# An MLP behind a layer norm: three tiles of the first block transposed before their normalisation, which moves behind the matmul as row and column corrections

## The chip, the cores and the metric

One core of a Trainium2 chip. The core has five engines that run side by side and meet at semaphores: TensorE (PE, matmuls, with its weight loads shown as PEld), VectorE (DVE), ScalarE (ACT), GpSimd (POOL) and SyncE (SP, which here only issues DMA transfers). The metric is device time in microseconds. Before the change the median of three runs is 398.32 us (398.21 to 398.36).

## The reference

```python
B, S, D, F = 1, 2048, 1024, 3584          # bfloat16 inputs

def _layernorm(x, axis=-1, eps=1e-5):
    m = jnp.mean(x, axis=axis, keepdims=True)
    v = jnp.var(x, axis=axis, keepdims=True)
    return (x - m) / jnp.sqrt(v + eps)

def reference(x, w1, b1, w2, b2):
    y = _layernorm(x, axis=-1)
    h = _gelu(jnp.einsum("bsd,df->bsf", y, w1) + b1)
    return jnp.einsum("bsf,fd->bsd", h, w2) + b2
```

## The kernel before

The 2048 rows of x are 16 tiles of 128, in four blocks of four tiles (512 rows). For each block the kernel normalises the four tiles, transposes them into yT_sb (model dimension on the partitions, eight chunks dt of 128), computes mm1, 28 rows r of 128 hidden units (eight matmuls of 512 columns each, summed in one bank of PSUM), applies gelu on ScalarE into hT_sb, and computes mm2, eight groups of 28 matmuls, which VectorE adds b2 to and SyncE stores. Blocks 1 to 3 are normalised and transposed by VectorE (in 32 by 32 pieces, L355) while TensorE works on the block before.

Block 0 has nothing to hide behind, and its opening is written out by hand. It is called the wave here: mm1 of the first seven rows, each in a PSUM bank of its own (ps_1 banks 0 to 4, ps_2 banks 1 and 0), taken in cells of one tile, one row and one chunk dt (128 columns), in an order that follows the arrival of tiles and weights. There are 4 x 7 x 8 = 224 cells (L415). Its transposes are done by TensorE (L378, 128 by 128, into a free bank) and copied to yT_sb by ScalarE (L385). The wave's order of cells and transposes comes from WAVE_K, T_PUTS and GROUPS; each engine runs its list in the order written. After the wave come rows 7 to 27 with 512 columns per matmul; row 7 is in the bank ps_t (which the transposes used before), row 8 in ps_1 bank 0, and so on round six banks, so that a row waits for the gelu of the row that had its bank.

Tile 0 is normalised in a special way: VectorE takes the statistics of its first half (L264), ScalarE sums its second half with one activation (L494), VectorE adds the two to four times the mean (L275) and writes 4x - 4m to o_sb (L281); tile 1 is centred by its mean alone (L286). TensorE starts on tile 0 then. For these two tiles the factor 1/deviation, a vector over rows of x and thus over columns of yT, is applied in PSUM: VectorE spreads it over the partitions by 16 small transposes (rbc_sb, L337) and multiplies 256 columns of each of block 0's 28 mm1 rows by it before the gelu (L425, dve_scale). Tiles 2 and 3 are normalised fully (L290), with the deviation's power of -1/2 on GpSimd (L268).

Until tile 0 is ready TensorE runs matmuls of ones (L490): 34 ungated, three behind tile 0's mean, and three more after the first five transposes. Loads go out on two queues: ScalarE's first issues x0's second half and all of x1; SyncE's issues x0's first half, then w0 to w5 (w1's rows 0 to 6, one 128-row chunk dt each, 224 KB), the halves of x2, w6, w7, the halves of x3, b1, and the larger rest.

A planner puts VectorE's later work in order before the launch: ops of `crit` (the scalings of block 0 and the additions of b2) and of `fill` (the next block's statistics and transposes) are merged by estimated due times, which start from T_DVE_START and T_PE_START. VectorE runs them in that order and waits at each for its semaphores.

Of the kernel before, what the change touches and what calls it, by code (L numbers as in the profile page):

```python
# [5 lines left out]
ACT = mybir.ActivationFunctionType  # L6
# [5 lines left out]
P = 128  # L12
# [3 lines left out]
K_GROUPS = 2  # L16
NB1 = 5
# [3 lines left out]
WARM_A = ((34, None), (3, "m4"))  # L21
WARM_B = 3
N_CENTRED = 2
T_PUTS = {0: (None, None, 6), 1: (21, 35), 2: (96, 118), 3: (140, 156)}
NORM = {0: (0, 2, 8), 1: (0, 4, 8), 2: (0, 4, 8)}
GROUPS_0 = (0, 2, 5, 8)
WAVE_ROWS_0 = 6
WAVE_K = (0, 2, 4, 5, 6, 8)
GROUPS_1 = (0, 4, 8)
# [61 lines left out]
def bass_standalone__mixer_channel_mlp__prompt_kernel(  # L91
# [53 lines left out]
    with ExitStack() as es:  # L145
# [67 lines left out]
        def issue(item):  # L213
            if item[0] == "x" and item[-1] in "ab":
# [44 lines left out]
        pool.op(lambda e: e.memset(b1r_sb[:, :], 0.0), sig="b1z")  # L259
        dve.op(lambda e: e.memset(st_sb[:, :, 12:14], 0.0))  # L260
# [6 lines left out]
        def op_aggr(i):  # L267
            pool.op(lambda e, i=i: e.tensor_tensor(out=rstd_sb[:, i:i + 1], in0=mv_sb[:, i, 1:2],  # L268
                                                   in1=nhalf[:, i:i + 1], op=ALU.pow),
                    waits=[f"mv{i}", "nhalf"], sig=f"rstd{i}")  # L270
            return (lambda e, i=i: e.bn_aggr(mv_sb[:, i, :], st_sb[:, i, :]),  # L271
                    [f"st{i}_0", f"st{i}_1", "eps"], f"mv{i}", 0.33)

        def op_mean0():
            return (lambda e: e.tensor_scalar(out=m4_sb[:, :], in0=st_sb[:, 0, 1:2], scalar1=st_sb[:, 0, 4:5],  # L275
                                              scalar2=half_sb[:, :], op0=ALU.add, op1=ALU.add),
                    ["st0_0", "half"], "m4", 0.1)

        def op_norm(i, c0, c1, sig):
            if i == 0:  # L280
                return (lambda e, c0=c0, c1=c1: e.tensor_scalar(  # L281
                            out=o_sb[:, 0, c0:c1], in0=x_sb[:, 0, c0:c1], scalar1=4.0,
                            scalar2=m4_sb[:, :], op0=ALU.mult, op1=ALU.subtract),
                        ["m4"], sig, 0.02 + (c1 - c0) * 0.00055)
            if i < N_CENTRED:
                return (lambda e, i=i, c0=c0, c1=c1: e.tensor_scalar(  # L286
                            out=x_sb[:, i, c0:c1], in0=x_sb[:, i, c0:c1], scalar1=mv_sb[:, i, 0:1],
                            scalar2=None, op0=ALU.subtract),
                        [f"mv{i}"], sig, 0.02 + (c1 - c0) * 0.00055)
            return (lambda e, i=i, c0=c0, c1=c1: e.tensor_scalar(  # L290
                        out=x_sb[:, i, c0:c1], in0=x_sb[:, i, c0:c1], scalar1=mv_sb[:, i, 0:1],
                        scalar2=rstd_sb[:, i:i + 1], op0=ALU.subtract, op1=ALU.mult),
                    [f"rstd{i}", f"mv{i}"], sig, 0.02 + (c1 - c0) * 0.00055)
# [3 lines left out]
        def ops_norm(i):  # L297
            cuts = NORM.get(i, (0, DT))
# [27 lines left out]
        def ops_rbc():  # L326
            res = []
            for i in range(N_CENTRED):
                res.append((lambda e, i=i: e.tensor_scalar(out=rq_sb[:, i, :], in0=ones[:, 0:32],
                                                           scalar1=rstd_sb[:, i:i + 1], scalar2=(1.0 if i else 0.25),  # L330
                                                           op0=ALU.mult, op1=ALU.mult),
                            ["ones", f"rstd{i}"], f"rq{i}", 0.1))
            for tq in range(4):
                for q in range(4):
                    src = rq_sb[32 * tq:32 * (tq + 1), :, :]
                    dst = rbc_sb[32 * q:32 * (q + 1), :, 32 * tq:32 * (tq + 1)]
                    res.append((lambda e, src=src, dst=dst: e.transpose(out=dst, in_=src), [f"rq{N_CENTRED - 1}"],  # L337
                                ("rbc" if tq == 3 and q == 3 else None), 0.1))
            return res
# [4 lines left out]
        def ops_T(i):  # L344
            blk, t = divmod(i, TPB)
            waits = [y_ev[i][-1]]
            if blk - 2 in mm1_done:
                waits.append(mm1_done[blk - 2])
            res = []
# [15 lines left out]
        t_banks = [("t", ps_t[:, 0, :]), ("2_0", ps_2b[:, 0, :]), ("t", ps_t[:, 0, :])]  # L365

        def pe_T(i, groups, k):
            blk, t = divmod(i, TPB)
            j0, j1 = groups[k], groups[k + 1]
            bname, bap = t_banks[k if i == 0 else 0]  # L370
            evs = yT_ev.setdefault(i, [None] * DT)
            for j in range(j0, j1):
                waits = []
                if j == j0:
                    waits = ["ident"] + ([bank_read[bname]] if bname in bank_read else [])
                if j == j0 or y_ev[i][j] != y_ev[i][j - 1]:
                    waits.append(y_ev[i][j])
                pe.op(lambda e, i=i, j=j, o=(j - j0) * P, bap=bap: e.transpose(  # L378
                    out=bap[:, o:o + P], in_=(x_sb[:, i] if i else o_sb[:, 0])[:, j * P:(j + 1) * P],
                    identity=ident[:, :]),  # L380
                    waits=waits, sig=(f"tp{i}_{k}" if j == j1 - 1 else None))
                evs[j] = f"te{i}_{k}"
            src = bap[:, 0:(j1 - j0) * P].rearrange("p (j s) -> p j s", j=j1 - j0)
            dst = yT_sb[:, blk % 2, j0:j1, t * P:(t + 1) * P]
            act.op(lambda e, dst=dst, src=src: e.copy(out=dst, in_=src), waits=[f"tp{i}_{k}"], sig=f"te{i}_{k}")  # L385
            bank_read[bname] = f"te{i}_{k}"
            pe_t[0] += (j1 - j0) * 0.056
# [240 lines left out]
```

## Time and profile before

| | |
|---|---|
| median of three runs | 398.32 us |
| span of the profiled execution, first to last instruction | 396.9 us |
| what lies around the span (median less span; the profile gives no other time of that execution) | 1.42 us |
| TensorE busy | 394.1 us (99%) |
| VectorE, ScalarE, GpSimd busy | 152.8, 82.8, 9.7 us |
| wave, first cell to row 7's first matmul | 5.92 to 20.00 us |
| mm2 of block 0, first matmul | 56.42 us |

A timeline row gives the start in us, the length in us, the engine, the line, the operation with its output and inputs, the count, and in brackets the idle time before it and what ended that. A row of the chain of waits gives start, length, engine, output tile, line and count. A row of a group gives line, engine, operation, shapes and count, then busy us and mean ns of one, then the idle time before. A DMA row gives what is moved, the queue, the count, the size and the us from issue to landing. A matmul's length includes its passage through the array, so the pace is read from starts.

### The profile page before, as it was taken

The numbers are of one execution on the slowest core, as the hardware profiler recorded it, in microseconds if no ns is written. First come the engines' busy times: TensorE is split into PE (matmuls) and PEld (weight loads), VectorE is DVE, ScalarE is ACT, GpSimd is POOL, SyncE is SP. The second block draws the span as 40 slices with busy tenths as digits, with TensorE's granted clock in tenths as the row PEclk, the third lists the DMA queues.
The fourth block names the chain that finished last, engine by engine and source line by source line (L and its number), as shares of the span: only waits on it lengthen the run. The fifth ranks groups of instructions, "written<-read, shape, count | busy, mean of one in ns | idle before, by whom it ended". The sixth has DMA issues, their size and how long they took to land.

```text
span 396.9 us, 4883 instructions
## 1 busy us (share of the span) xinstructions
PE 394.1 (99%) x2116; PEld 191.7 (48%) x2116; DVE 152.8 (38%) x345; ACT 82.8 (21%) x124; POOL 9.7 (2%) x24
## 2 busy tenths in 40 slices
PE   9999999999999999999999999999999999999998
PEld 8944444444444444444444444444444444444447
DVE  5847899989998005988100000001100000001011
ACT  4273430000133442000024433100003334400000
POOL 2101000020002000000000000000000000000000
PEclk9999999999999999999999999999999999999999
DMA  8999940000000000000000000000000000000000
GB/s 286 347 380 384 387 154 13 26 29 13 26 2 0 2 0 1 28 13 26 28 13 0 2 0 2 13 13 28 16 24 15 0 0 2 0 13 28 13 28 26
DMA packets 16924, 23.64 MB, mean 60 GB/s; under 512 B 1672, under 2 KB 10504, under 8 KB 16904
## 3 DMA queue, kind: packets, MB, share of 16 engines
q1 hardware_dynamic: 16616, 22.95, 16.4%
q8 instruction: 16, 0.26, 0.3%
q10 hardware_dynamic: 288, 0.39, 0.3%
q14 instruction: 4, 0.03, 0.0%
HBM read 19.14 MB, written 4.19 MB: 59 GB/s over the span
## 4 chain that ended last, share of the span: by engine, by line
PE 99%; ACT 0%; DVE 0%; issue 0%
PE ps L466 49%; PE ps L415 41%; PE ps_t L415 8%; PE ps L490 1%; PE ps_t L378 0%; ACT yT_sb L385 0%; DVE o_sb L477 0%
## 5 line engine op out<-in xcount | busy, mean ns | idle before, releaser
L466 PE MATMUL ps<-w_sb,hT_sb 128*128 128x512 bf16 (+1 forms) x980 | 194.2, 361 | 0.0
L415 PE MATMUL ps<-yT_sb,w_sb 128*128 128x512 bf16 (+1 forms) x920 | 167.4, 340 | 0.1
L466 PEld LDWEIGHTS ps<-w_sb,hT_sb 128*128 128x128 bf16 x980 | 91.3, 98 | 102.7
L415 PEld LDWEIGHTS ps<-yT_sb,w_sb 128*128 128x128 bf16 x920 | 80.9, 98 | 82.5 <-issue 0.3
L432 ACT ACTIVATE hT_sb<-ps,b_sb 128x512 bf16<-128x512 f32 x94 | 64.0, 688 | 237.2 <-PE ps L415 217.1
L477 DVE TENSOR_TENSOR o_sb<-ps,b_sb 128x512 bf16<-128x512 f32 (+1 forms) x35 | 22.6, 646 | 198.2 <-PE ps L466 198.1
L355 DVE STREAM_TRANSPOSE yT_sb<-x_sb 32x256 bf16<-32x256 bf16 x192 | 83.7, 436 | 26.6 <-PE ps_t L415 23.5
L415 PE MATMUL ps_t<-yT_sb,w_sb 128*128 128x512 bf16 x144 | 34.0, 379 | 0.0
L264 DVE BATCH_NORM_STATS2 st_sb<-x_sb 128x6 f32<-128x512 bf16 x32 | 21.1, 674 | 4.9 <-DMA x_sb<-in_x_dram 4.9
L415 PEld LDWEIGHTS ps_t<-yT_sb,w_sb 128*128 128x128 bf16 x144 | 14.0, 98 | 16.8
L432 ACT ACTIVATE hT_sb<-ps_t,b_sb 128x512 bf16<-128x512 f32 x18 | 12.4, 690 | 17.0 <-PE ps_t L415 14.6
L425 DVE TENSOR_TENSOR ps<-ps,rbc_sb 128x256 f32<-128x256 f32 x24 | 9.7, 426 | 6.1 <-PE ps L415 5.9
L268 POOL TENSOR_TENSOR rstd_sb<-mv_sb,nhalf 128x1 f32<-128x1 f32 x16 | 8.9, 559 | 118.7 <-DVE mv_sb L271 118.7
L290 DVE TENSOR_SCALAR x_sb<-x_sb,mv_sb,rstd_sb 128x1024 bf16<-128x1024 bf16 (+1 forms) x15 | 7.8, 525 | 3.9 <-POOL rstd_sb L268 3.3
L385 ACT COPY yT_sb<-ps_t 128x512 bf16<-128x512 bf16 (+2 forms) x8 | 4.4, 545 | 8.1 <-PE ps_t L378 8.1
L490 PE MATMUL ps<-const-bfloat16-1.0 128*128 128x128 bf16 x40 | 4.6, 302 | 0.8 <-PEq L613 0.8
L490 PEld LDWEIGHTS ps<-const-bfloat16-1.0 128*128 128x128 bf16 x40 | 4.0, 139 | 1.0 <-issue 0.8
L271 DVE BATCH_NORM_AGGREGATE mv_sb<-st_sb 128x2 f32<-128x15 f32 x16 | 3.5, 221 | 1.3
L337 DVE STREAM_TRANSPOSE rbc_sb<-rq_sb 32x64 f32<-32x64 f32 x16 | 3.8, 236 | 0.2
L378 PE MATMUL ps_t<-ident,x_sb 128*128 128x128 bf16 x24 | 2.3, 219 | 0.0
L425 DVE TENSOR_TENSOR ps_t<-ps_t,rbc_sb 128x256 f32<-128x256 f32 x4 | 1.6, 405 | 0.1
L493 ACT ACT_TABLE_LOAD x1 | 1.3, 1283 | 1.7 <-PEq L613 1.7
(24 smaller groups left out, 8.0 us busy)
## 6 DMA issues: line engine op xcount, KB each, us to landing
w_sb<-in_w_dram SPq DMA_DIRECT2D x4, 1792.0 KB, 18.3
out_dram<-o_sb SPq DMA_DIRECT2D x31, 128.0 KB, 1.7
x_sb<-in_x_dram SPq DMA_DIRECT2D x3, 1024.0 KB, 14.1
w_sb<-in_w_dram SPq DMA_DIRECT2D x2, 1024.0 KB, 9.1
w_sb<-in_w_dram SPq DMA_DIRECT2D x1, 2048.0 KB, 15.2
w_sb<-in_w_dram SPq DMA_DIRECT2D x8, 224.0 KB, 4.7
w_sb<-in_w_dram SPq DMA_DIRECT2D x1, 1280.0 KB, 14.7
x_sb<-in_x_dram SPq DMA_DIRECT2D x5, 128.0 KB, 4.6
```

The costliest lines, as they stand in the source:

```text
L264: return (lambda e, i=i, h=h: e.bn_stats(st_sb[:, i, 6 * h:6 * (h + 1)], x_sb[:, i, h * HC:(h + 1) * HC]), [x_ev[i][h]], f"st{i}_{h}", 0.65)
L268: pool.op(lambda e, i=i: e.tensor_tensor(out=rstd_sb[:, i:i + 1], in0=mv_sb[:, i, 1:2], in1=nhalf[:, i:i + 1], op=ALU.pow), waits=[f"mv{i} ...
L290: return (lambda e, i=i, c0=c0, c1=c1: e.tensor_scalar(out=x_sb[:, i, c0:c1], in0=x_sb[:, i, c0:c1], scalar1=mv_sb[:, i, 0:1], scalar2=rst ...
L337: res.append((lambda e, src=src, dst=dst: e.transpose(out=dst, in_=src), [f"rq{N_CENTRED - 1}"], ("rbc" if tq == 3 and q == 3 else None), ...
L355: res.append((lambda e, src=src, dst=dst: e.transpose(out=dst, in_=src), waits, (f"tr{i}" if lastop else None), 0.47))
L385: act.op(lambda e, dst=dst, src=src: e.copy(out=dst, in_=src), waits=[f"tp{i}_{k}"], sig=f"te{i}_{k}")
L415: pe.op(lambda e, b=b, r=r, dt=dt, n0=n0, n1=n1, bank=bank: e.matmul(unit_bank(bank)[:, n0:n1], lhsT=w1_sb[:, dt, r * P:(r + 1) * P], rhs= ...
L425: crit.append((est[wait_ev], (lambda e, ap=ap: e.tensor_tensor(out=ap, in0=ap, in1=rbc_sb[:, :, :].rearrange("p t s -> p (t s)"), op=ALU.m ...
L432: act.op(lambda e, r=r, n0=n0, n1=n1, bank=bank: e.activation(out=hT_sb[:, r, n0:n1], in_=unit_bank(bank)[:, n0:n1], func=ACT.Gelu_apprx_tanh,
L466: pe.op(lambda e, st=st, ft=ft, c0=c0, c1=c1, bank=bank: e.matmul(ps_2[:, bank, 0:c1 - c0], lhsT=hT_sb[:, ft, st * P:(st + 1) * P], rhs=w2 ...
L477: crit.append((est[sig], (lambda e, ob=ob, c0=c0, c1=c1, bank=bank: e.tensor_tensor(out=o_sb[:, ob, c0:c1], in0=ps_2[:, bank, 0:c1 - c0], ...
L490: pe.op(lambda e: e.matmul(ps_1[:, 0, 0:P], lhsT=unit, rhs=unit, start=True, stop=True), waits=[gate] if gate else [])
```

## The change

Tiles 0, 1 and 2 of block 0 are transposed raw, without statistics, each in two halves of four chunks, into the second buffer of yT_sb (`yT_sb[:, 1]`, block 1's), tile 3 normalised as before into the first. A column of ones stands behind the three tiles' 384 columns there, so that a matmul of 385 columns also gives the sum of the weights over the model dimension for each hidden unit, c. With r the vector 1/deviation and m the mean over rows of x, the wanted sum is (raw - c m) r for these three tiles.

For the wave this is done in PSUM: ScalarE copies c out of column 384 (act_cs) before tile 3's cells add to that column; VectorE takes two passes over 385 columns of each of the seven rows (ops_corr): add c times the row vector -m, then multiply by the row vector r. The row vectors are made by VectorE (five small operations, ops_rows, which split -m and r into three bf16 parts; four transposes of 32 rows by 192 columns, ops_rvt) and spread over the partitions by one matmul of 384 columns each (pe_row), which ScalarE copies to row_sb. For rows 7 to 27, VectorE writes the three tiles centred (raw - m) to the first buffer (ops_fix, three additions of 128 by 1024), and dve_scale multiplies 384 columns of PSUM by r, in place of 256. Row 7 takes tile 3's 128 columns first, then the other 384. Block 1's transposes into the second buffer wait for the wave's last raw cell and the fixes.

The 40 ones-matmuls become 24, ungated. ScalarE's queue first loads the first halves of x1 and x2; SyncE's loads x0's first half, w0, w1, then the second halves of x0, x1 and x2 as one transfer (xrb), w2 to w4, x3's halves, w5 to w7. Gone are the half sum on ScalarE, tile 0's and 1's own centring and the 16 small transposes. GpSimd gets six memsets more, and one power over three columns in place of three.

```diff
-WARM_A = ((34, None), (3, "m4"))
-WARM_B = 3
-N_CENTRED = 2
+WARM = 24
+N_RAW = 3
+RC = N_RAW * P
-SP_FIRST_LOADS = ("x0a", "w0", "w1", "w2", "w3", "w4", "w5", "x2a", "x2b", "w6", "w7", "x3a", "x3b", "b1", "w8")
-ACT_FIRST_LOADS = ("x0b", "x1")
-T_PE_START = 5.7
-T_DVE_START = 16.5
+SP_FIRST_LOADS = ("x0a", "w0", "w1", "xrb", "w2", "w3", "w4", "x3a", "x3b", "w5", "w6", "w7", "b1", "w8")
+ACT_FIRST_LOADS = ("x1a", "x2a")
+T_PE_START = 4.2
+T_DVE_START = 26.0
...
+        def ops_rows():
+            return [(lambda e: e.tensor_scalar(out=rv_sb[:, 0:N_RAW], in0=mv_sb[:, 0:N_RAW, 0], scalar1=-1.0,
+                                               scalar2=None, op0=ALU.mult),
+                     ["rstdr"] + [f"mv{i}" for i in range(N_RAW)], "nmr", 0.15),
+                    (lambda e: e.tensor_copy(rv3_sb[:, :, 0], rv_sb[:, :]), ["nmr", "rv0"], "rhi", 0.15),
+                    (lambda e: e.tensor_tensor(out=rr_sb[:, :], in0=rv_sb[:, :], in1=rv3_sb[:, :, 0], op=ALU.subtract),
+                     ["rhi"], "rr1", 0.15),
+                    (lambda e: e.tensor_copy(rv3_sb[:, :, 1], rr_sb[:, :]), ["rr1"], "rmid", 0.15),
+                    (lambda e: e.tensor_tensor(out=rv3_sb[:, :, 2], in0=rr_sb[:, :], in1=rv3_sb[:, :, 1],
+                                               op=ALU.subtract), ["rmid"], "rlo", 0.15)]
+        def ops_rvt():
+            return [(lambda e, q=q: e.transpose(out=rvt_sb[0:32, :, 32 * q:32 * (q + 1)],
+                                                in_=rv3_sb[32 * q:32 * (q + 1), :, :]),
+                     ["rlo", "rvt0"], ("rvt" if q == 3 else None), 0.35) for q in range(4)]
...
+        def ops_fix(i):
+            s0, s1 = i * P, (i + 1) * P
+            return [(lambda e: e.tensor_tensor(out=yT_sb[:, 0, :, s0:s1], in0=yT_sb[:, 1, :, s0:s1],
+                                               in1=row_sb[:, 0:1, s0:s1].to_broadcast([P, DT, P]), op=ALU.add),
+                     ["row0", f"te{i}_0", f"te{i}_1"], f"fx{i}v", 1.25)]
...
+        head = [op_stats(i, h) for h in range(2) for i in raw] + [op_aggr(i) for i in raw]
+        pool.op(lambda e: e.tensor_tensor(out=rv_sb[:, N_RAW:2 * N_RAW], in0=mv_sb[:, 0:N_RAW, 1], in1=nhalf[:, 0:N_RAW],
+                                          op=ALU.pow),
+                waits=[f"mv{i}" for i in raw] + ["nhalf"], sig="rstdr")
+        head += [op_stats(N_RAW, 0), op_stats(N_RAW, 1), op_aggr(N_RAW)] + ops_rows() + ops_rvt() + ops_norm(N_RAW)
...
+        def ops_corr(r):
+            ap = unit_bank(wave[r][0])[:, 0:RC + 1]
+            return [(lambda e: e.scalar_tensor_tensor(out=ap, in0=row_sb[:, 0, :], scalar=cs_ap[r], in1=ap,
+                                                      op0=ALU.mult, op1=ALU.add),
+                     [f"m1_0_{r}", cs_ev[r], "row0", "row1c"], f"sa_{r}", 0.62),
+                    (lambda e: e.tensor_tensor(out=ap, in0=ap, in1=row_sb[:, 1, :], op=ALU.mult),
+                     [f"sa_{r}", "row1"], f"sb_{r}", 0.56)]
...
+        def pe_row(k):
+            pe.op(lambda e: e.matmul(ps_tf[:, 0, 0:RC], lhsT=sel_sb[:, :],
+                                     rhs=rvt_sb[:, k * N_RAW:(k + 1) * N_RAW, :].rearrange("p v s -> p (v s)"),
+                                     start=True, stop=True), waits=["sel", "rvt", bank_read["t"]], sig=f"pr{k}")
+            act.op(lambda e: e.copy(out=row_sb[:, k, 0:RC], in_=ps_tf[:, 0, 0:RC]), waits=[f"pr{k}", "row1c"],
+                   sig=f"row{k}")
...
+        first, most, every = range(NB1), [*range(NB1), R - 1], range(R)
+        pe_T([(0, 0)], "t")
+        pe_T([(1, 0)], "2_0")
+        cells(first, (0,), 0, 1)
+        pe_T([(2, 0)], "2_1")
+        cells(first, (0,), 1, 2)
+        cells((R - 1,), (0,), 0, 2)
+        cells(most, (1,), 0, 2)
+        cells((NB1,), (0, 1), 0, 2)
+        pe_T([(0, 1), (1, 1)], "t")
+        cells(every, (0, 1), 2, 3)
+        cells(every, (2,), 0, 3)
+        pe_T([(2, 1)], "t")
+        cells(every, (3,), 0, 3)
+        cells(first, range(4, DT - 1), 0, 3)
+        pe_row(0)
+        cells(first, (DT - 1,), 0, 3)
+        act_cs(ps_1, 0, NB1, False)
+        last2 = range(NB1, R)
+        cells(last2, (4,), 0, 3)
+        pe_T([(3, 0), (3, 1)], "t")
+        cells(last2, range(5, DT), 0, 3)
+        act_cs(ps_2, NB1, R, True)
+        r4 = R // 2 + 1
+        late_cells(3, range(r4), range(h))
+        pe_row(1)
+        late_cells(3, range(r4), range(h, DT))
+        late_cells(3, range(r4, R), range(DT))
+        for o in corr:
+            dve_put(o)
...
-                mm1_row(b, r)
+                mm1_row(b, r, ((N_RAW, TPB), (0, N_RAW)) if b == 0 and r == r0 else ((0, TPB),))
```

More of the change, by code (lines that the diff above doesn't have):

```diff
@@ L364, in bass_standalone__mixer_channel_mlp__prompt_kernel @@
         bank_read = {}
[L365 to L387, printed above, removed]
@@ new lines, in cells @@
+        def cells(rows, dts, t0, t1, by_row=False):
+            n0, n1 = t0 * P, t1 * P + (1 if t1 == N_RAW else 0)
+            order = [(r, dt) for r in rows for dt in dts] if by_row else [(r, dt) for dt in dts for r in rows]
+            for r, dt in order:
+                bank = wave[r][0]
+                w = [yT_ev[i][dt] for i in range(t0, t1)] + (["rone"] if n1 > RC else [])
+                if r not in started:
+                    w += [bank_read[k] for k in (f"{bank[0]}_{bank[1]}",) if k in bank_read]
+                pe_cell(r, dt, 1, n0, n1, bank, w, f"cw_{r}" if dt == DT - 1 and n1 > RC else None,
+                        r not in started, False, shared=True)
+                started.add(r)
```

214 lines of the change are left out of this document (108 added, 106 removed).

## The prediction

> **What bounds the kernel now.** I read the page's first, second and fourth parts, then TensorE's timeline, then the chain of waits over the opening.
>
> ```profile
> span 396.9 us, 4883 instructions
> PE 394.1 (99%) x2116; PEld 191.7 (48%) x2116; DVE 152.8 (38%) x345; ACT 82.8 (21%) x124; POOL 9.7 (2%) x24
> PEclk9999999999999999999999999999999999999999
> PE 99%; ACT 0%; DVE 0%; issue 0%
> ...
> 0.82 4.26 PE L490 MATMUL ps<-const-bfloat16-1.0 128*128 128x128 bf16 x37 [0.82 <-PEq L613]
> ...
> 0.82 2.72 PE L490 MATMUL ps<-const-bfloat16-1.0 128*128 128x128 bf16 x24 [0.82 <-PEq L613]
> 4.99 0.37 PE L378 MATMUL ps_t<-ident,o_sb 128*128 128x128 bf16 x2
> 5.23 0.37 PE L378 MATMUL ps<-ident,o_sb 128*128 128x128 bf16 x3
> 5.44 0.33 PE L490 MATMUL ps<-const-bfloat16-1.0 128*128 128x128 bf16 x3
> 5.92 0.49 PE L415 MATMUL ps<-yT_sb,w_sb 128*128 128x128 bf16 x6
> 20.00 1.89 PE L415 MATMUL ps_t<-yT_sb,w_sb 128*128 128x512 bf16 x8
> ...
> 8.72 3.41 PE ps L415 x61
> 21.89 8.63 PE ps L415 x40
> ```
>
> The chain is TensorE for 99% of the span. Row 7 begins at 20.00, and all behind it is TensorE's own pace, so the change is worth what it moves that 20.00, unless it makes a new stall later. The last two rows (start, length, count) give the paces: 3.41/61 = 0.0559 us for a matmul of 128 columns, 8.63/40 = 0.2158 for 512. From 5.92 to 20.00 run 224 cells and the 27 transposes that are left of 32: 251 x 0.0559 = 14.03 of 14.08 us. The wave is full; only its start, after x0's first statistics, can be gained.
>
> The second of these timeline rows is cut out of the first and holds 24 warm-up matmuls in 2.72 us, a pitch of 0.107 with the last one's passage of some 0.3 on top. By 5.92 the pitch is (6.25 - 5.92)/6 = 0.055. Between 5.23 and 5.44 three transposes take 0.07 each: TensorE doubles its pace at about 5.3, 4.5 us after its first matmul. The granted clock shows 9 tenths or more from the first slice on, so this is read from the pace alone.
>
> **What the change does to the wave's start.** Tile 0 is transposed as soon as its first half lands. Durations come from the one profiled execution, whose span is 396.90; the shown runs' median, 398.32, lies 1.42 above it, and I add that at the end.
>
> ```profile
> 0.78 0.38 SPq L190 DMA_DIRECT2D x_sb<-in_x_dram  x1
> 1.22 2.79 SPq L190 DMA_DIRECT2D w_sb<-in_w_dram  x6
> 4.05 0.97 SPq L190 DMA_DIRECT2D x_sb<-in_x_dram  x2
> ...
> x_sb<-in_x_dram ACTq DMA_DIRECT2D x1, 128.0 KB, 2.6
> x_sb<-in_x_dram SPq DMA_DIRECT2D x1, 128.0 KB, 2.4
> ...
> w_sb<-in_w_dram SPq DMA_DIRECT2D x1, 224.0 KB, 3.3
> ...
> w_sb<-in_w_dram SPq DMA_DIRECT2D x1, 224.0 KB, 4.6
> ...
> w_sb<-in_w_dram SPq DMA_DIRECT2D x1, 224.0 KB, 4.8
> ...
> x_sb<-in_x_dram SPq DMA_DIRECT2D x1, 128.0 KB, 4.6
> ...
> 5.40 0.37 ACT L385 COPY yT_sb<-ps_t 128x256 bf16<-128x256 bf16 x1 [1.26 <-PE ps_t L378]
> 5.67 0.48 ACT L385 COPY yT_sb<-ps 128x384 bf16<-128x384 bf16 x1
> 7.68 0.58 ACT L385 COPY yT_sb<-ps_t 128x512 bf16<-128x512 bf16 x1 [0.58 <-PE ps_t L378]
> ```
>
> The first three rows are SyncE's issues, 0.47 us each. The DMA rows behind them, each from a window that holds the one or two issues shown, end with the time to landing. The first loads of both queues, issued at 0.78, land at 3.2 and 3.4: the change puts the first halves of x0 and x1 there. w0 (issued at 1.22) lands at 4.5. w2 (2.15) lands at 6.7, with 1184 KB asked for up to it on both queues; w4 (3.10) at 7.9 with 1632 KB; tile 2's second half (4.59) at 9.2 with 2112 KB. The new order asks for 1216 KB up to xrb and for 2144 KB up to tile 3's second half, which puts them at 6.8 and 9.3; it moves w2 to w7 behind xrb, by 32 to 256 KB (0.1 to 0.7 us), and each is needed over 0.7 us after that. From w8 on the bytes ahead are the same. Three second halves hang on xrb's one signal. If it came without w2's slow last pieces it would be 6.2 (halfway from w0's 4.5 to w4's 7.9 at an even pace); if as late as w4, 7.9.
>
> The 24 warm-ups last until 3.38; eight transposes at 0.107 end at 4.23. Tile 0's four are through at 4.01 (0.3 of passage), ScalarE copies 512 columns in 0.58, and a cell starts 0.15 after a copy's end (5.40 + 0.37 to 5.92): 4.78. Five cells at 0.107 reach 5.31 (w0 is there at 4.5), where I let the pace double. Then, at 0.0559 per 128 columns and, between the 128 and 512 paces by a straight line, 0.109 per 256 and 0.163 per 385: four transposes 0.22, five cells 0.28, seven 256-wide 0.76, two more 0.22, so 6.8, just when xrb is due. Eight transposes 0.45, fourteen cells of 129 0.79, seven of 385 1.14, four transposes 0.22, 22 of 385 3.59: 13.0. The ends for a 385 are the 256 and 512 values, 0.109 and 0.216; I keep the line, since nothing in the rows sets an odd width apart, and 0.216 would cost 42 x 0.053 = 2.2 us.
>
> **The row matmul and what feeds it.** At 13.0 the queue meets the first row matmul, which waits for VectorE; every cell of the wave stands behind it.
>
> ```profile
> 3.25 0.70 DVE L264 BATCH_NORM_STATS2 st_sb<-x_sb 128x6 f32<-128x512 bf16 x1 [2.27 <-DMA x_sb<-in_x_dram]
> 5.09 1.28 DVE L264 BATCH_NORM_STATS2 st_sb<-x_sb 128x6 f32<-128x512 bf16 x2
> 6.47 0.22 DVE L271 BATCH_NORM_AGGREGATE mv_sb<-st_sb 128x2 f32<-128x15 f32 x1
> 14.08 0.55 DVE L290 TENSOR_SCALAR x_sb<-x_sb,mv_sb,rstd_sb 128x1024 bf16<-128x1024 bf16 x1 [0.66 <-POOL rstd_sb L268]
> 14.54 0.20 DVE L323 STREAM_TRANSPOSE b1t_sb<-b1r_sb 128x32 bf16<-128x32 bf16 x1
> 14.78 0.18 DVE L324 CAST b_sb<-b1t_sb 128x28 f32<-128x28 bf16 x1
> 15.29 3.98 DVE L337 STREAM_TRANSPOSE rbc_sb<-rq_sb 32x64 f32<-32x64 f32 x16
> L355 DVE STREAM_TRANSPOSE yT_sb<-x_sb 32x256 bf16<-32x256 bf16 x192 | 83.7, 436 | 26.6 <-PE ps_t L415 23.5
> ...
> 10.58 0.55 POOL L268 TENSOR_TENSOR rstd_sb<-mv_sb,nhalf 128x1 f32<-128x1 f32 x1 [1.74 <-DVE mv_sb L271]
> ```
>
> Statistics come every 0.60 us (two in 1.28). Three second halves from 6.85, three aggregates (0.22 each, 0.14 apart) until 9.1, tile 3's two halves until 10.4 (its second lands at 9.3, in time), its aggregate at 10.5. GpSimd's power over three columns starts at 9.1 and costs 0.55, at most 3 x 0.55: 10.75, hidden or 0.15 late. Then five dependent operations on six columns. The nearest row is the 0.18 cast, which began 0.04 after the transpose that it needed: 0.22 each, 1.1 in all; the ends are 5 x 0.19 = 0.95 without that gap and 5 x 0.32 = 1.6 with the aggregate's 0.22 and the 0.1 it began after its statistics (5.09 + 1.28 to 6.47). Four transposes of 192 columns: 0.20 for 32, 0.24 for 64 (3.98/16 = 0.25 apart) and 0.44 for 256 lie on a line that gives 0.37, 0.38 apart, 1.52; ends 1.0 and 1.8. So VectorE is ready at 10.6 + 1.1 + 1.5 = 13.2, TensorE 0.15 later, **13.37**, a wait of 0.35; the ends give 12.7 and 14.1.
>
> Behind it stand 2 row matmuls (0.325), 13 cells of 385 (2.12), 8 transposes and 56 cells of 128 (3.58): 6.02 us. Row 7 starts at **19.39** in place of 20.00. Its split into 128 and 384 columns costs 8 x (0.0559 + 0.1625 - 0.2158) = 0.02. Sum: 396.90 - 0.61 + 0.02 = 396.31 for the span, and with the 1.42 **397.7**.
>
> **What is counted at nothing, and its cover.**
>
> ```profile
> 23.65 0.43 DVE L425 TENSOR_TENSOR ps<-ps,rbc_sb 128x256 f32<-128x256 f32 x1 [1.29 <-PE ps L415]
> 31.20 0.69 DVE L264 BATCH_NORM_STATS2 st_sb<-x_sb 128x6 f32<-128x512 bf16 x1 [1.94 <-DMA x_sb<-in_x_dram]
> 75.31 2.70 DVE L355 STREAM_TRANSPOSE yT_sb<-x_sb 32x256 bf16<-32x256 bf16 x6
> 104.61 5.34 PE L415 MATMUL ps<-yT_sb,w_sb 128*128 128x512 bf16 x24
> L432 ACT ACTIVATE hT_sb<-ps,b_sb 128x512 bf16<-128x512 f32 x94 | 64.0, 688 | 237.2 <-PE ps L415 217.1 <-DVE ps L425 20.1
> L477 DVE TENSOR_TENSOR o_sb<-ps,b_sb 128x512 bf16<-128x512 f32 x31 | 21.4, 692 | 193.5 <-PE ps L466 193.4
> ```
>
> Tile 3's transposes follow the row matmul by 1.3 us; ScalarE's copy of the row (0.5) and tile 3's scaling (0.55) fit under that. The three fixes start at 14.1, after the row and b1; one is between L290's 0.55 and two of L477's 0.69 = 1.38; at about 1.15 they end at 17.6, and row 7's second part asks for them at 19.8. Uncovered, they would have to take 1.9 each.
>
> The seven corrections queue behind the fixes on VectorE. Each is two dependent passes over 385 PSUM columns; 0.43 for 256 and 0.69 for 512 give 0.56, with 0.04 of start 1.2 a row, 8.4 in all, until about 26. Row 8 needs bank 1_0, thus row 0's gelu: 17.6 + 1.2 + 0.69 = 19.5 against 21.1. Later rows ask every 1.73 and get one every 1.2. Row 13 needs row 7's bank, whose scaling stands behind all seven: 26.6 + 0.7 against 29.8. Even two passes of 0.69 (1.46 a row) would make that 29. Then VectorE waits for block 1's load (31.20) as before, the wider scalings cost 0.13 each more, and block 1's transposes, which end near 78 now, end some 6 us later against 104.61. GpSimd's six memsets, the dropped half sum on ScalarE, the new waits of block 1's transposes and the shared buffer lie far from any need.
>
> **The rivals.**
> A, VectorE's rows come first. If the small operations are at their low ends or xrb lands at 6.2, TensorE never waits: 13.03 + 6.02 = 19.05, 397.4; with both xrb and the pace early, down to 396.9. For it: the middle estimate is only 0.35 behind. Against: every dependent row above has a start gap.
>
> B, the pace doubles late. The change takes 13 warm-ups and the three fillers away, and TensorE stands from 4.23 to 4.78. Where the count of busy time starts anew at 4.78 and again takes 4.5 us, the pace is half from 5.3 until 9.3: 4.0 us do the work of 2.0. TensorE comes to the row matmul at 15.0, which swallows the wait for VectorE, and row 7 starts at 21.05: **399.4**. B decides from a doubling after about 7.2, where row 7 is back at 20.0. Against it: 37 warm-ups in 4.26 us are 0.3 more than their pitch, so TensorE had gaps before too, and the pace rose.
>
> The Trainium skill bears on B ("TensorE: Matmul & The Clock Gate", Part 1 on the clock gate and Part 4 on the transpose): the gate judges free-running windows of about 3.4 us, and transposes do not count as busy time in the same way. By it eight transposes and a gap would make this window look less than full, and the next one ends 3.4 us later, at about 8.7: an estimate of 399.1 by that page. The trace agrees with a rise after some 4 us; no row here shows what transposes count for.
>
> C, xrb is late. Landing at 7.9 (w4's place), it holds TensorE and the statistics together by 1.1 us: row 7 at 20.5, 398.8. It decides from 7.4 on. Against it: its bytes are w2's plus 32 KB.
>
> **How the numbers follow.** The forecast (VectorE's rows hold TensorE until about 13.4) has 0.37, its own range 397.4 to 398.5 by the ends above; A 0.32, B 0.19, C 0.12. I take 0.2%, 0.8 us, as what a measurement can tell from no change: the bounds are 397.5 and 399.1. Faster: nine tenths of A and a fifth of the forecast, 0.36. Slower: four fifths of B and a little of C, 0.17. The rest, 0.47, is the same. The range runs from A's low end to B's figure, 396.9 to 399.4.
>
> **What would show it.** Right: the first transposes near 3.4, first cells near 4.8, a TensorE gap before the first row matmul that VectorE's 32-row transposes end, row 7 near 19.4, and no TensorE wait after it. Wrong: no such gap (A), cells still 0.107 apart after 6 (B), the eight transposes waiting for xrb past 7 (C), or a row after 7 waiting for a bank.

## The result and the profile after

| | before | after |
|---|---|---|
| median of 13 runs each | 398.47 us (398.21 to 398.67) | 397.62 us (397.32 to 397.91) |
| ratio of after to before, 95% interval | | 0.998 (0.9972 to 0.9988) |
| span of the profiled execution | 396.9 us | 396.4 us |
| first cell of the wave | 5.92 us | 4.77 us |
| row 7's first matmul | 20.00 us | 19.43 us |

The kernel became 0.2% faster, 0.5 to 1.1 us by the interval. The profiled executions differ by 0.5 us. The changed kernel's runs lie 1.2 to 1.3 us above their spans (the profiled one 397.62 to 396.4).

The page's first lines, its chain by engine and line, and TensorE's timeline of the opening (start, length, line, operation, count, idle before):

```profile
span 396.4 us, 4688 instructions
PE 393.4 (99%) x2017; PEld 187.8 (47%) x2017; DVE 160.6 (41%) x340; ACT 83.4 (21%) x125; POOL 9.8 (2%) x28
PE 98%; DMA 1%; SPq 0%; DVE 0%; issue 0%
...
0.82 2.72 PE L491 MATMUL ps<-const-bfloat16-1.0 128*128 128x128 bf16 x24 [0.82 <-PEq L680]
3.51 0.58 PE L383 MATMUL ps_t<-ident,x_sb 128*128 128x128 bf16 x4
4.77 0.64 PE L415 MATMUL ps<-yT_sb,w_sb 128*128 128x128 bf16 x5 [0.25 <-ACT yT_sb L391]
5.25 0.39 PE L383 MATMUL ps<-ident,x_sb 128*128 128x128 bf16 x4
5.47 1.66 PE L415 MATMUL ps<-yT_sb,w_sb 128*128 128x128 bf16 x14
7.11 0.62 PE L383 MATMUL ps_t<-ident,x_sb 128*128 128x128 bf16 x8
9.73 3.76 PE L415 MATMUL ps<-yT_sb,w_sb 128*128 128x385 bf16 x22
13.41 0.32 PE L564 MATMUL ps_t<-rvt_sb,sel_sb 128*128 128x384 bf16 x1
17.19 2.40 PE L415 MATMUL ps<-yT_sb,w_sb 128*128 128x128 bf16 x40
19.43 1.91 PE L415 MATMUL ps_t<-yT_sb,w_sb 128*128 128x128 bf16 x16
21.17 8.80 PE L415 MATMUL ps<-yT_sb,w_sb 128*128 128x512 bf16 x40
```

The chain now has 1% of DMA in it, which it had not before. The wave begins 1.15 us earlier and ends 0.57 earlier. The chain of waits over the opening, in order of time (start, length, what), shows where one half of the difference went, and the two DMA rows (size, us from issue to landing) are the transfers concerned:

```profile
1.70 4.34 DMA w_sb<-in_w_dram
6.04 0.05 issue
6.08 1.05 PE ps L415 x8
7.13 0.60 PE ps_t L383 x8
7.73 1.94 PE ps L415 x21
9.67 0.22 PE ps_t L383 x4
9.89 3.59 PE ps L415 x22
...
w_sb<-in_w_dram SPq DMA_DIRECT2D x1, 224.0 KB, 4.3
...
x_sb<-in_x_dram SPq DMA_DIRECT2D x1, 384.0 KB, 4.9
```

w1 lands at 6.04, where it landed at 5.45 before. The 14 cells of the timeline's row at 5.47 are five of 128 columns and nine of 256, 1.26 us at the predicted paces; until the transposes of 7.11 they take 1.64. The first six are through at 5.86 (5 x 0.056 + 0.109 from 5.47) and the seventh starts at 6.08: 0.23 us for w1. The remaining 0.15 is the wait for xrb, which lands at 7.07 (2.16 + 4.9) in place of 6.8. At the first row matmul the wait is small: 22 cells at 0.163 (3.59 / 22) from 9.73 end at 13.32, and the row matmul starts at 13.41. These three waits (0.23, 0.15 and 0.09) and the half pace of the first five cells (0.48 us from 4.77 to 5.25, in place of 0.28) make 0.67 us. The work from the first cell to row 7 is some 0.1 shorter than before at full pace (by the pitches 7.95 us up to the first row matmul and 6.02 behind it, 13.97 against 14.08), which leaves about the 0.58 that the earlier start gives back.

VectorE in the same stretch, and GpSimd's power over three columns:

```profile
7.09 1.88 DVE L271 BATCH_NORM_STATS2 st_sb<-x_sb 128x6 f32<-128x512 bf16 x3 [1.64 <-DMA x_sb<-in_x_dram]
9.21 1.29 DVE L271 BATCH_NORM_STATS2 st_sb<-x_sb 128x6 f32<-128x512 bf16 x2
10.74 0.10 DVE L283 TENSOR_SCALAR rv_sb<-mv_sb 128x3 f32<-128x3 f32 x1
11.76 1.51 DVE L294 STREAM_TRANSPOSE rvt_sb<-rv_sb 32x192 bf16<-32x192 bf16 x4
14.28 3.50 DVE L339 TENSOR_TENSOR yT_sb<-yT_sb,row_sb 128x1024 bf16<-128x1024 bf16 x3
17.69 0.62 DVE L540 SCALAR_TENSOR_TENSOR ps<-row_sb,cs_sb,ps 128x385 f32<-128x385 f32 x1
18.82 0.61 DVE L540 SCALAR_TENSOR_TENSOR ps<-row_sb,cs_sb,ps 128x385 f32<-128x385 f32 x1
25.57 0.56 DVE L548 TENSOR_TENSOR ps_t<-ps_t,row_sb 128x384 f32<-128x384 f32 x1
83.53 1.29 DVE L271 BATCH_NORM_STATS2 st_sb<-x_sb 128x6 f32<-128x512 bf16 x2
...
9.44 0.88 POOL L498 TENSOR_TENSOR rv_sb<-mv_sb,nhalf 128x3 f32<-128x3 f32 x1 [6.79 <-DVE mv_sb L279]
```

The statistics wait for xrb until 7.09; from there to 13.27, the end of the four transposes, VectorE has no gap but its start gaps. So two chains, TensorE's own and VectorE's, start at xrb's landing and meet at 13.3 to 13.4 within 0.1 us: TensorE's takes 6.21 us from there (7.11 to 13.32), VectorE's 6.32 (7.09 to 13.41, with the 0.14 between its last transpose and the row matmul). The questions for the experiments: is it such a tie, what do the transfers cost, how much room have the fixes, and what does the pace of the first microseconds depend on.

### The profile page after: what moved, and what is told of

It is laid out like the page before. It is cut to its first block, busy times and chain, and to the rows that moved or that the text cites. A ratio compares the mean times of both kernels' runs of the same rounds, so it can differ in the third digit from the quotient of the medians.

```text
span 396.4 us, 4688 instructions
## 1 busy us (share of the span) xinstructions
PE 393.4 (99%) x2017; PEld 187.8 (47%) x2017; DVE 160.6 (41%) x340; ACT 83.4 (21%) x125; POOL 9.8 (2%) x28
## 4 chain that ended last, share of the span: by engine, by line
PE 98%; DMA 1%; SPq 0%; DVE 0%; issue 0%
PE ps L467 49%; PE ps L415 41%; PE ps_t L415 8%; DMA w_sb<-in_w_dram 1%; PE ps_t L383 0%; SPq L185 0%; PE ps_t L564 0%; DVE o_sb L478 0%
## 5 line engine op out<-in xcount | busy, mean ns | idle before, releaser
L415 PE MATMUL ps<-yT_sb,w_sb 128*128 128x512 bf16 (+4 forms) x827 | 167.3, 360 | 0.3 <-ACT yT_sb L391 0.3
L415 PEld LDWEIGHTS ps<-yT_sb,w_sb 128*128 128x128 bf16 x827 | 77.6, 98 | 85.5 <-ACT yT_sb L391 0.5
L415 PE MATMUL ps_t<-yT_sb,w_sb 128*128 128x512 bf16 (+2 forms) x152 | 34.0, 368 | 0.0
L548 DVE TENSOR_TENSOR ps<-ps,row_sb 128x384 f32<-128x384 f32 x17 | 9.4, 565 | 4.7 <-PE ps L415 4.5
L299 DVE TENSOR_SCALAR x_sb<-x_sb,mv_sb,rstd_sb 128x1024 bf16<-128x1024 bf16 x13 | 7.0, 541 | 1.9 <-POOL rstd_sb L276 1.3
L540 DVE SCALAR_TENSOR_TENSOR ps<-row_sb,cs_sb,ps 128x385 f32<-128x385 f32 x7 | 4.3, 615 | 0.0
L391 ACT COPY yT_sb<-ps_t 128x512 bf16<-128x512 bf16 x6 | 3.3, 588 | 4.3 <-PE ps_t L383 4.3
L543 DVE TENSOR_TENSOR ps<-ps,row_sb 128x385 f32<-128x385 f32 x7 | 4.0, 567 | 0.2
L339 DVE TENSOR_TENSOR yT_sb<-yT_sb,row_sb 128x1024 bf16<-128x1024 bf16 x3 | 3.5, 1222 | 0.1
L548 DVE TENSOR_TENSOR ps_t<-ps_t,row_sb 128x384 f32<-128x384 f32 x4 | 2.3, 564 | 0.9 <-PE ps_t L415 0.8
```

The source lines that it names most:

```text
L299: return (lambda e, i=i, c0=c0, c1=c1: e.tensor_scalar(out=x_sb[:, i, c0:c1], in0=x_sb[:, i, c0:c1], scalar1=mv_sb[:, i, 0:1], scalar2=rst ...
L415: pe.op(lambda e: e.matmul(unit_bank(bank)[:, n0:n1], lhsT=w1_sb[:, dt, r * P:(r + 1) * P], rhs=yT_sb[:, buf, dt, n0:n1], start=start, sto ...
L540: return [(lambda e: e.scalar_tensor_tensor(out=ap, in0=row_sb[:, 0, :], scalar=cs_ap[r], in1=ap, op0=ALU.mult, op1=ALU.add), [f"m1_0_{r}" ...
L543: (lambda e: e.tensor_tensor(out=ap, in0=ap, in1=row_sb[:, 1, :], op=ALU.mult), [f"sa_{r}", "row1"], f"sb_{r}", 0.56)]
L548: crit.append((est[wait_ev], (lambda e: e.tensor_tensor(out=ap, in0=ap, in1=row_sb[:, 1, 0:RC], op=ALU.mult), [wait_ev, "row1"], f"sc_{r}" ...
```

## The experiments

Each kernel is the changed kernel with the edit shown, and is compared with the kernel before on the same chip. The kernel before had medians of 398.35 to 398.49 us in the four groups of runs. The changed kernel was run once more:

> The changed kernel once more, beside the runs of this group on the same chip. Both theories: 397.6 us within 0.15.

Measured: 397.65 us (397.44 to 398.38, 11 runs), ratio 0.9984 (0.9975 to 0.9992). The changed kernel's runs spread over 0.6 us in the first series and 0.9 in this one, so differences of 0.2 us between medians are at the edge of what these runs tell. In its second profile the two chains meet again: the 22 cells end at 13.20 (9.61 + 3.59), the four transposes at 13.20, the row matmul starts at 13.35 and row 7 at 19.36.

**VectorE's rows made sooner.**

```diff
-                    (lambda e: e.tensor_copy(rv3_sb[:, :, 0], rv_sb[:, :]), ["nmr", "rv0"], "rhi", 0.15),
...
-                                               op=ALU.subtract), ["rmid"], "rlo", 0.15)]
+                    (lambda e: e.tensor_copy(rv3_sb[:, :, 0], rv_sb[:, :]), ["nmr", "rv0"], "rlo", 0.15)]
```

> The second and third bf16 parts of the row vectors are left out: three of VectorE's five small operations go, so its rows are ready 0.66 us earlier (three times 0.22). Theory (tie): in the changed kernel TensorE waits only 0.09 us for VectorE at the first row matmul (last cell begun at 13.16, +0.163, row matmul at 13.41), because it had lost 0.28 us before at w1 and 0.2 at xrb; so row 7 starts 0.1 earlier and the time stays within 0.1 to 0.2 us of the changed kernel's 397.6. Rival (VectorE's rows set the end, as forecast): row 7 up to 0.35 or more earlier, about 397.2.

Measured: 397.44 us (397.23 to 397.76, 8 runs), ratio 0.9977 (0.9967 to 0.9987). TensorE's timeline of this kernel:

```profile
9.70 3.76 PE L410 MATMUL ps<-yT_sb,w_sb 128*128 128x385 bf16 x22
13.29 0.33 PE L559 MATMUL ps_t<-rvt_sb,sel_sb 128*128 128x384 bf16 x1
```

In its trace the row matmul starts at 13.29, directly behind the 22 cells, and row 7 at 19.31: 0.12 earlier than in the changed kernel, from rows that were ready 0.65 earlier (12.62 against 13.27). The tie holds; the full 0.35 of the forecast's wait was not there.

**VectorE's rows made later.**

```diff
-                                               op=ALU.subtract), ["rmid"], "rlo", 0.15)]
+                                               op=ALU.subtract), ["rmid"], "rlo0", 0.15)] + [
+                    (lambda e: e.tensor_copy(rr_sb[:, :], rv_sb[:, :]), [f"rlo{k}"], f"rlo{k + 1}" if k < 2 else "rlo", 0.15)
+                    for k in range(3)]
```

> Three more dependent small operations (copies into a scratch tile) stand before the four row transposes on VectorE: 0.66 us later. Theory (tie): only 0.09 us of slack the other way is there, so nearly all of it is paid: row 7 at about 20.0 (19.43 + 0.66), 398.3 us, the gain over the kernel before gone. Rival (the transfers alone set the wave's end and VectorE has room): under 0.2 us, 397.8 or less.

Measured: 398.44 us (398.08 to 398.7, 11 runs), ratio 1.0 (0.9991 to 1.0008): 0.8 us slower than the changed kernel, the whole gain. TensorE's timeline of this kernel:

```profile
9.46 3.76 PE L417 MATMUL ps<-yT_sb,w_sb 128*128 128x385 bf16 x22
14.50 0.32 PE L566 MATMUL ps_t<-rvt_sb,sel_sb 128*128 128x384 bf16 x1 [1.28 <-DVE rvt_sb L296]
```

TensorE waits 1.28 us for the transposes. In this execution xrb came early (the cells begin at 9.46, not 9.73) and tile 3's first half late (it landed at 9.66, against 9.18 in the changed kernel), which adds to the wait; it is also the slowest of the eleven runs. The medians give the price of the edit. Shorter by 0.66 gained 0.1 to 0.2, longer by 0.66 cost 0.8, which is the whole 0.66 within the spread of the runs: VectorE's chain was at the point where it begins to set the end.

**The second halves in three transfers.**

```diff
-SP_FIRST_LOADS = ("x0a", "w0", "w1", "xrb", "w2", "w3", "w4", "x3a", "x3b", "w5", ...
+SP_FIRST_LOADS = ("x0a", "w0", "w1", "x0b", "x1b", "x2b", "w2", "w3", "w4", "x3a", "x3b", "w5", ...
```

> The three second halves come as three transfers with a signal each, in place of one. Theory (xrb's last piece at 7.07 holds TensorE for 0.2 us and all of VectorE's statistics): the first half lands near 6.3 and the third near 7.1; TensorE's eight transposes no longer wait or wait less, VectorE's statistics end 0.6 or more earlier until tile 3's second half (9.5) holds them, rows ready 0.25 earlier: row 7 0.2 to 0.3 earlier, 397.3 to 397.4. Rival (two more issues of 0.47 us on SyncE push w2 and all behind it later, and the last halves land no earlier): no gain or up to 0.3 us slower.

Measured: 397.43 us (397.05 to 397.75, 10 runs), ratio 0.9977 (0.9968 to 0.9986), by medians 0.2 under the changed kernel. VectorE of this kernel:

```profile
5.64 1.88 DVE L271 BATCH_NORM_STATS2 st_sb<-x_sb 128x6 f32<-128x512 bf16 x3 [0.17 <-DMA x_sb<-in_x_dram]
8.67 1.29 DVE L271 BATCH_NORM_STATS2 st_sb<-x_sb 128x6 f32<-128x512 bf16 x2 [0.86 <-DMA x_sb<-in_x_dram]
```

The first of the three lands at 5.62, sooner than expected, and the last at 6.42; then VectorE waits 0.86 us for tile 3. TensorE's transposes start at 6.53 without a wait, the row matmul at 12.87 after one of 0.13, row 7 at 18.89. This execution is the fastest of the ten (397.05).

**The same, with tile 3 ahead of w3 and w4.**

```diff
+SP_FIRST_LOADS = ("x0a", "w0", "w1", "x0b", "x1b", "x2b", "w2", "x3a", "x3b", "w3", "w4", "w5", ...
```

> The second halves come as three transfers, and tile 3's two halves go ahead of w3 and w4. With the split alone VectorE sat 0.86 us for tile 3's first half (statistics at 8.67) and TensorE 0.13 us for the row matmul. Theory: tile 3 lands by about 7.8, the rows are ready by 12.0, TensorE finds them ready at its own 12.7; w3 (needed at 9.1) and w4 (10.4) land by 8.6 and 9.2, in time. Row 7 near 18.75, 397.3 us, 0.1 below the split alone and 0.3 below the changed kernel. Rival (the transfers' jitter, not VectorE, sets what is left, or w3 comes late): no better than the split alone, 397.4 to 397.6.

> The split with tile 3 ahead of w3, once more: its eight runs fell in two groups, 396.94 to 397.22 and 397.68 to 397.86. Theory (the time at which the pace doubles differs from run to run; the profiled run had it by 5.1, the slow group later): the same two groups, 0.5 to 0.8 us apart. Rival (chance): one group about 397.45.

Measured: 397.45 us (396.94 to 397.86, 8 runs), ratio 0.9975 (0.9965 to 0.9985), and again 397.4 us (397.01 to 397.92, 10 runs), ratio 0.9974 (0.9965 to 0.9983). TensorE of the first:

```profile
12.76 0.33 PE L564 MATMUL ps_t<-rvt_sb,sel_sb 128*128 128x384 bf16 x1
18.78 1.91 PE L415 MATMUL ps_t<-yT_sb,w_sb 128*128 128x128 bf16 x16
```

The row matmul follows the cells with no wait, 0.65 us earlier than in the changed kernel, and row 7 starts at 18.78. That is the profiled run, one of 396.94, the fastest of its series, as is the profiled one of the second (397.01); the median gained little over the split alone. Of the 18 runs eight lie above 397.6 and ten at 397.41 or below, and no trace shows one of the eight. In both profiles VectorE's rows come first; what decides between the two groups isn't shown.

**Fillers in the gap before the first cells.**

```diff
         pe_T([(1, 0)], "2_0")
+        warm(4)
         cells(first, (0,), 0, 1)
```

This is the kernel just above with four matmuls of ones.

> Four matmuls of ones stand in TensorE's wait between tile 1's transposes and the first cells (4.13 to 4.69), where the kernel before had its fillers. At 0.107 each they end by 4.6, before ScalarE's first copy is through, so they cost nothing themselves. Theory (the gap helps to make the pace double late in some runs): the slow group of the split grows rarer or vanishes, median 397.0 to 397.2. Rival (the two groups come from the transfers, or from a window whose place does not depend on the gap): median and spread as without fillers.

> The fillers once more: in six runs none was above 397.45, where 8 of 18 runs of the same kernel without them were above 397.6. Theory (the fillers take the late doubling away): again all under 397.5, median 397.0 to 397.3. Rival (chance): about four runs in ten above 397.6.

Measured: 397.25 us (396.92 to 397.45, 6 runs), ratio 0.9969 (0.9957 to 0.9981), and again 397.49 us (396.87 to 397.87, 11 runs), ratio 0.9977 (0.9968 to 0.9986). Five of the second eleven lie above 397.6. The theory of the fillers fell with the second series; what parts the two groups of its runs stays open. In the second one's profile the first cells wait for a transfer, not for the pace:

```profile
5.08 0.44 PE L415 MATMUL ps<-yT_sb,w_sb 128*128 128x128 bf16 x5 [0.55 <-DMA w_sb<-in_w_dram]
```

**w1 on the other queue.**

```diff
-SP_FIRST_LOADS = ("x0a", "w0", "w1", "xrb", "w2", ...
-ACT_FIRST_LOADS = ("x1a", "x2a")
+SP_FIRST_LOADS = ("x0a", "w0", "xrb", "w2", ...
+ACT_FIRST_LOADS = ("x1a", "x2a", "w1")
```

> w1 goes third on ScalarE's queue in place of third on SyncE's, so it shares the engines with w0 and xrb. Theory (w1's last piece at 6.04 costs TensorE 0.28 us, which the wait for xrb and the rows then mostly takes back): w1 lands by 5.4, no wait there, but xrb at about the same time, so TensorE waits 0.5 for xrb: row 7 within 0.1 us, 397.5 to 397.7. Rival (w1's late piece is what sets the wave's end): the whole 0.28 is gained, 397.3.

Measured: 398.77 us (397.82 to 402.09, 12 runs), ratio 1.0026 (1.0006 to 1.0046), 1.1 us slower than the changed kernel, which neither theory had. w1's DMA row and TensorE's wait:

```profile
w_sb<-in_w_dram ACTq DMA_DIRECT2D x1, 224.0 KB, 5.7
...
7.50 1.05 PE L415 MATMUL ps<-yT_sb,w_sb 128*128 128x256 bf16 x8 [1.69 <-DMA w_sb<-in_w_dram]
```

The ratio stands above that of the medians (1.001) because four of the twelve runs took 400.7 us or more; their granted clock is 0.991 to 0.996, where every other run here shows 1.000. In the profile the transfer takes 5.7 us in place of 4.3, lands at 7.45, and TensorE stands 1.69 us. Eight of its sixteen pieces had landed by 5.62 and fifteen by 6.91. From 4.6 to 5.6 us, with most of these pieces still under way, ScalarE's queue moved 0.13 MB and SyncE's 0.21: beside SyncE's long list it got less than half. No order within SyncE's queue that was tried here cost as much.

**xrb later (rival C).**

```diff
-SP_FIRST_LOADS = ("x0a", "w0", "w1", "xrb", "w2", "w3", ...
+SP_FIRST_LOADS = ("x0a", "w0", "w1", "w2", "xrb", "w3", ...
```

> In the changed kernel's order xrb goes behind w2 (224 KB, some 0.6 us later). Theory (rival C of the prediction: xrb's landing moves TensorE's eight transposes and VectorE's statistics together): w2 lands at 6.0, xrb at 7.5 to 7.7, rows and row 7 0.4 to 0.6 us later, 398.0 to 398.2. Other theory (VectorE is held by tile 3's landing and TensorE by w1, xrb has room): within 0.15 us of 397.6.

Measured: 398.1 us (397.81 to 398.68, 11 runs), ratio 0.9994 (0.9986 to 1.0003), 0.45 slower. TensorE and VectorE of this kernel:

```profile
7.67 0.62 PE L383 MATMUL ps_t<-ident,x_sb 128*128 128x128 bf16 x8 [0.79 <-DMA x_sb<-in_x_dram]
...
7.65 1.88 DVE L271 BATCH_NORM_STATS2 st_sb<-x_sb 128x6 f32<-128x512 bf16 x3 [1.94 <-DMA x_sb<-in_x_dram]
```

Both engines wait for the one signal and start within 0.02 us of each other: xrb moves both chains, as C had it. It lands 0.55 later than in the changed kernel (7.65 against 7.1 at VectorE), and 0.45 of that is paid.

**Fewer ones-matmuls (rival B).**

```diff
-WARM = 24
+WARM = 12
```

> Twelve of the 24 ungated ones-matmuls are left out; TensorE stands from 2.1 to 3.4 us. This tells what brings the doubling of the pace (5.2 us in the changed kernel). Theory (a stretch of some 3 to 4 us in which TensorE is nearly always busy is needed): the pace doubles only after 7 us, the opening's 5 cells, 20 transposes and the first wide cells take twice as long; less what the waits for w1, xrb and the rows swallow (0.6 us), 0.5 to 1.3 us slower than the changed kernel, 398.1 to 398.9, and more spread between runs. Rival (what counts is the time since the first matmul, or any matmul): doubling near 5 as before, within 0.15 us of 397.6.

Measured: 398.77 us (397.83 to 399.21, 10 runs), ratio 1.0008 (0.9998 to 1.0017), 1.1 us slower than the changed kernel. TensorE of this kernel:

```profile
3.42 0.58 PE L383 MATMUL ps_t<-ident,x_sb 128*128 128x128 bf16 x4 [1.17 <-DMA x_sb<-in_x_dram]
4.68 0.72 PE L415 MATMUL ps<-yT_sb,w_sb 128*128 128x128 bf16 x5 [0.25 <-ACT yT_sb L391]
5.62 2.66 PE L415 MATMUL ps<-yT_sb,w_sb 128*128 128x128 bf16 x14
8.07 1.06 PE L383 MATMUL ps_t<-ident,x_sb 128*128 128x128 bf16 x8
8.93 2.30 PE L415 MATMUL ps<-yT_sb,w_sb 128*128 128x129 bf16 x21
11.06 0.39 PE L383 MATMUL ps_t<-ident,x_sb 128*128 128x128 bf16 x4
```

The eight transposes start 0.107 apart ((8.93 - 8.07)/8), four later ones 0.055. The 21 cells between them take 2.13 us (8.93 to 11.06) where full pace gives 1.93, so some four of them ran at half pace: the pace doubles only near 9.3. Row 7 starts at 20.90 in this execution, close to the 21.05 that B's sum gave for a doubling at 9.3, and B's price is seen: 1.5 us in the trace, 1.1 by medians. The matmuls of ones are needed, the idle stretch from 2.1 to 3.4 puts the doubling off, by 3 us or more against every profile with 24, and time since the first matmul alone does not bring it.

**The fixes done twice.**

```diff
-                     ["row0", f"te{i}_0", f"te{i}_1"], f"fx{i}v", 1.25)]
+                     ["row0", f"te{i}_0", f"te{i}_1"] + [f"fx{i}u"] * (k == "v"), f"fx{i}{k}", 1.25) for k in "uv"]
```

> Each of the three fixes on VectorE is done twice (the second writes the same values once more). Theory (cover of the fixes: they end at 17.7 and row 7's second part asks at 19.9, 2.2 us of room): six take 7.5 us from 14.3, end at 21.8; TensorE waits 2.0 us inside row 7 and then some 0.4 for row 0's gelu behind the later corrections: 2.2 to 2.6 us slower than the changed kernel, 399.8 to 400.2. Rival (the corrections' queue on VectorE is further from need than that, or the fixes are not waited for): under 0.5 us.

Measured: 399.86 us (399.77 to 400.14, 5 runs), ratio 1.0037 (1.0024 to 1.005), 2.2 slower than the changed kernel. VectorE and TensorE of this kernel:

```profile
14.23 7.28 DVE L339 TENSOR_TENSOR yT_sb<-yT_sb,row_sb 128x1024 bf16<-128x1024 bf16 x6
...
21.66 1.46 PE L415 MATMUL ps_t<-yT_sb,w_sb 128*128 128x384 bf16 x8 [1.67 <-DVE yT_sb L339]
23.65 3.62 PE L415 MATMUL ps<-yT_sb,w_sb 128*128 128x512 bf16 x16 [0.54 <-ACT hT_sb L424]
```

3.8 us more of fixes put row 7's second part off by 1.8 us (to 21.66, from 19.83 by the pace) and cost 2.2 in all: the cover named in the prediction is there and has about the size it gave (3.8 less 1.8, 2.0 against 2.2), and with it used up the next wait is for row 0's gelu, as the queue of corrections would have it.

## Why the prediction was right

The forecast was 397.7 us and the measured median is 397.62. The chain that it named ends last: VectorE's rows are what the first row matmul waits for, at 13.41, and nothing holds TensorE later. The size of that wait it had too large, and the figure is nearer than its terms deserved. By its steps:

- The start. First transpose 3.51 (3.38 predicted), first cell 4.77 (4.78), pace doubled at the first cells, near 5.2 (5.3), in this execution.
- xrb at 7.07 in place of 6.8. A wait for w1 (0.23 us, last piece at 6.04) was not in the prediction, which took every chunk of w1 to be in time. It cost little, since TensorE would else have stood longer at xrb.
- VectorE's chain. Five small operations 1.02 us (1.1 predicted), four transposes 1.51 (1.52), ready at 13.27 (13.2), row matmul at 13.41 (13.37). GpSimd's power took 0.88, inside its bounds, and was hidden, ending at 10.32 before 10.74.
- The wait at the row matmul was to be 0.35 and is 0.09 (0.15 in the second profile). TensorE came to it 0.3 later than summed (13.32 against 13.0), held by w1 and xrb; VectorE's part from xrb to the end of the transposes took 6.18 us (7.09 to 13.27) in place of 6.35 (6.85 to 13.2). That a later xrb and a shorter chain add up to 13.41, so near to 13.37, is luck. The price of the rows is thus a tie of two chains and not a bound by one; the short and the long rows show both sides of it.
- Behind it, 6.02 us to row 7 (13.41 to 19.43), as summed, with 0.163 for 385 columns: an odd width costs what the straight line says. Row 7 in two parts takes 1.74 (21.17 - 19.43), 0.02 over 1.725. The first matmul of block 0's mm2 moves from 56.26 to 55.71, so what row 7 gained is kept.
- The cover. The fixes take 3.50 and end at 17.78 (17.6), wanted at 19.88; a corrected row takes 1.13 (18.82 - 17.69; 1.2 predicted); row 7's scaling starts at 25.57 and holds nobody; block 1's transposes end before 83.53, 5.5 us later than before (6 predicted) and 20 us before need.
- The base. The 1.42 us that the prediction added to the span was too large by 0.1 to 0.2. Beside the experiments, runs of the kernel before with a span of 396.9 took 398.14 to 398.20 us, 1.2 to 1.3 above it, as after the change; the rest of the 1.42 is that the profiled execution was shorter than the median one. So the profiles, 0.5 us apart, understate the change: the medians differ by 0.85, with 0.5 to 1.1 as the interval, where the prediction had 0.6.

Of its signs of being wrong, C's came true by a little: the eight transposes start at 7.11, after a wait of 0.15 for xrb, which landed 0.27 late. And the gap at the row matmul is so small that the timeline does not mark it as idle, which is near to A's sign. No later row waits for a bank.

The rivals: A's case (rows ready first) is what the split with tile 3 ahead makes of the kernel, row 7 at 18.78 and its lowest run at 396.94, and not what the changed kernel does.

B's mechanism is real, as the twelve matmuls of ones show, and with 24 of them it comes in a mild form: the last matmul at half pace starts at 5.06 in the changed kernel's profile, at 3.2 in its second one, and as late as 6.0 in the trace of the fixes done twice. The prediction had one sample, 5.3, and took it for a fixed time; 7.2, from which B decides, was not reached. Its argument against B was weaker than it says: 37 pitches of 0.107 are 3.96 of the 4.26 us, and 0.2 of the other 0.3 is the passage of the last matmul beyond its pitch, so the warm-ups of the kernel before had a gap of 0.1 us only.

The Trainium skill ("TensorE: Matmul & The Clock Gate", Part 1) has the pace rise at the end of a busy window of some 3.4 us whose place does not follow the kernel's start; a rise that moves from 3.2 to 6.1, and one at 9.3 behind an idle stretch, agree with a place that is not fixed. The rise at 3.2 to 3.5 came 2.4 to 2.7 us after the first matmul, though, sooner than a whole busy window of that length. Its Part 4, by which transposes do not count in the same way, was not borne out as a danger: the 3.4 us before the late rise at 6.1 hold twelve transposes at 0.107, over a third of the stretch, and the pace rose. No run separates whether they count.

C's mechanism is real too, 0.45 us for one transfer further back.

No kernel here is clearly faster than the changed one. The split with tile 3 ahead is 0.2 to 0.25 us lower by medians in two series, within the spread of single runs.

## What to carry to other kernels

When an opening is pulled forward, list what each later step waits for on every queue: here an earlier start of 1.15 us was worth 0.57, the rest went to three waits that had been hidden behind the old start (0.47 us) and to first cells at half pace (0.2). Two chains that end within 0.1 us of each other hide each other's price: shorten one and little comes of it, lengthen it and all is paid, so test both directions before calling either the bound. Transfers that feed two engines may want their own signals, in the order of need within one queue; here that was worth about 0.2 us by medians, at the edge of what the runs tell.

## What the runs showed of the hardware

One piece of sixteen can hold a transfer: w1's landing of 6.04 is its last piece, and the other fifteen were there by 5.20; in the six profiles with the changed kernel's order w1 lands anywhere from 5.23 to 6.04. The x halves that came one by one landed at 5.6 to 6.0 (the first) and 6.4 to 6.7 (the last) in five profiles, where the joint transfer came between 6.51 and 7.07 in six. A transfer third on ScalarE's queue, beside SyncE's list, took 5.7 us for 224 KB against 4.3 as third on SyncE's, with runs of that kernel up to 402.09 us. The time at which TensorE's pace doubles differs from one execution to the next by up to 2.9 us (3.2 to 6.1) with the same 24 ones-matmuls ahead. The first two rows below are the changed kernel's second profile: the first transposes are 0.06 apart on average ((3.73 - 3.49)/4, with 3.73 the start of the next four), and the first cells wait for w0. The other two, from the kernel with the fixes done twice, are four transposes at 0.107 and the fourteen cells behind them, which take 1.49 us (to 7.16) where full pace gives 1.26, so four or five of them ran at half pace:

```profile
3.49 0.40 PE L383 MATMUL ps_t<-ident,x_sb 128*128 128x128 bf16 x4
4.93 0.44 PE L415 MATMUL ps<-yT_sb,w_sb 128*128 128x128 bf16 x5 [0.82 <-DMA w_sb<-in_w_dram]
```

```profile
5.24 0.63 PE L383 MATMUL ps<-ident,x_sb 128*128 128x128 bf16 x4
5.67 1.66 PE L415 MATMUL ps<-yT_sb,w_sb 128*128 128x128 bf16 x14
```

That alone is up to 1.4 us of TensorE's work in an opening, less what waits swallow, and it may have a part in the spread between runs of one kernel; no run shows that. In the two profiles of the changed kernel a rise 1.9 us earlier was worth 0.07 us at row 7 (19.36 against 19.43), since w0, xrb and VectorE's rows took the rest back.
